# Block-sparse attention and routed experts on one core: sparse weighing one tick later, and three early weight subtractions moved from GpSimd to VectorE

## The chip, the cores and the metric

The kernel runs on 1 core of one Trainium2 chip. The metric is the device time of one execution in microseconds (us), smaller being better. The kernel before was timed three times: 539.57 us is the median, 537.37 and 539.88 us the ends.

## What is computed

Attention with a block mask, followed by a layer of eight experts of which each token uses one. The shapes are q, k, v of 4 x 8 x 768 x 64 and, for the experts, 3072 tokens of 512 numbers, eight pairs of weights of 512 x 1024 and 1024 x 512, all in fp32.

```
scores = (q @ k^T) / 8                     # per batch and head, 768 x 768
mask   = |blk_i - blk_j| <= 1, or blk_i or blk_j is the first or last block,
         or blk_j is one of 3 sampled blocks of blk_i          # blocks of 32
x      = softmax(scores where mask) @ v    # -> 3072 tokens x 512
logits = x @ w_gate + modality_bias[modality_id]
e      = argmax(logits);  g = softmax(logits)[e]
out    = g * (relu(x @ w1[e]) @ w2[e])
```

## The kernel before

**Attention, by items and ticks.** The queries of the first and last block see all keys; they make 16 dense items (`"d"`, one of a batch and a pair of heads each). All others see eight blocks of 32 keys; they make 88 sparse items (`"s"`). Four sparse items (two places n, two batches b) make one tile of 128 tokens, so there are 22 sparse tiles, here called tile 0 to tile 21. The items stand in one list, `items`, of NI = 104. Each goes through steps named by a letter, and a table `LAG` (line 59) says how many ticks after its place in the list an item's step is written into the program:

- S, scores on TensorE (line 532, two items at once); M, mask and row minimum on VectorE (line 540); X, exponentials on ScalarE (line 548); T, four transposes on TensorE (line 557); A, copy of the transposes out of PSUM on ScalarE (line 562).
- For the last item of a tile only: W, the products with the values that all four items share, on TensorE (line 579); V, the row sums (line 572) and the products with each item's own three sampled blocks (line 588); O, the division that copies the output tile `xr` out of PSUM on VectorE (lines 439 to 441); Y, four transposes of that tile (line 595) with a copy on ScalarE (line 597); G, the gate's products (line 605), after which the tokens are routed and the tile is written to DRAM (line 1221).

The order within a tick is the string `ORDER` (line 60): O X T S M G V A Y W. There is no other scheduler: each engine executes in the order that this loop writes, and semaphores hold it where data or a buffer is missing. `hook` (line 1186) is called at eight places of a tick and issues the loads: the values of a tile (`fetch_v`, line 484, at `VL`; `fetch_own`, line 510, at `VG`) go through the one queue of SyncE (SP), and `share_v` (line 499) copies values between the two value buffers on GpSimd.

**Early weights.** Once 16 of the 24 tiles of tokens are routed, a first group of 256 tokens of one expert is chosen, and the generator `early_groups` (line 787) is advanced once a tick beside the attention. It loads pieces of that expert's weights in halves of 256 KB (line 710) into staging buffers and splits each piece in two: ScalarE copies it with rounding to fp32r (`split`, line 721), and a subtraction gives the rest (line 722). `POOL_SPLITS` (line 80) lists the pieces whose subtraction goes to GpSimd instead of VectorE. Pieces 0, 1 and 2 are split at ticks 6, 9 and 12 of that generator, and pieces 3 and 4 after the attention's last loads. Each product with weights is three matmuls (high by high, high by low, low by high), lines 746 to 748 and 761 to 763.

**Experts.** Groups of 256 tokens follow each other: gather by indirect DMA (line 728), transposes (line 735), first layer, ReLU, second layer, scatter (line 782). The first group's products start as soon as the last attention products are issued.

Of the kernel before, what the change touches and what calls it, by code (L numbers as in the profile page):

```python
# [9 lines left out]
F32 = mybir.dt.float32  # L10
# [5 lines left out]
ALU = mybir.AluOpType  # L16
# [5 lines left out]
B, H, S, D = 4, 8, 768, 64  # L22
# [33 lines left out]
START_TICKS = 14  # L56
DENSE_DVE = ((0, 0), (0, 1))
DENSE_AFTER = (21, 29, 45, 47)
LAG = {'d': {'S': 0, 'M': 1, 'X': 2, 'T': 4, 'A': 4, 'W': 7, 'O': 8, 'V': 101, 'Y': 11, 'G': 13}, 's': {'S': 0, 'M': 1, 'X': 2, 'T': 4, 'A': 4, 'W': 5, 'V': 7, 'O': 8, 'Y': 10, 'G': 13}}
ORDER = 'OXTSMGVAYW'  # L60
ADVANCE = (((2, 3), (6, 6), (7, 1)), ((0, 2), (1, 1), (6, 4)))
LHS = (6, 5)
# [3 lines left out]

KL = (-2, 2)
QP = (-2, 2)
VL = (8, 1)
VS = (11, 7)  # L70
VG = ((9, 6), (10, 3))

DENSE_IN = ((19, 14, 30), (49, 38, 44))
Q_IN = 22
# [2 lines left out]
XD = (7, 7)  # L77
TAIL = 7
EVAC_DVE = ()
POOL_SPLITS = (1, 2, 4, 7, 15, 16, 21)  # L80

TICKS = (6, 9, 12)
DOWN0 = ((9, 5), (9, 7), (14, 7), (12, 9), (13, 9), (13, 9), (17, 9), (15, 10))
# [5 lines left out]
def attention_moe(ctx, tc, kD, qD, qH, v0, v1, blocks, modality, w_gate, bias, w1, w2, out):  # L89
    nc = tc.nc  # L90
# [28 lines left out]
    with ExitStack() as actx:  # L119
# [529 lines left out]
        stg, wh, wl, xg, xh, xl, hh, hl, og = [], [], [], [], [], [], [], [], []  # L649
# [40 lines left out]
        NSTG, NRING, LOOK_D, LOOK_S = 5, 5, 6, 4  # L690
# [9 lines left out]
        def staged(n):  # L700
            return stg[(0, 1, 0, 1, 0, 1, 0, 2)[n] if n < 8 else n % NSTG]
# [14 lines left out]
                src = w2[bass.ds(e, 1), 2 * c * P:(2 * c + 2) * P, :].rearrange("e (k p) f -> p (e k) f", p=P)  # L716
                nc.sync.dma_start(staged(n).rearrange("p (k f) -> p k f", k=2), src)

        def split(n, eng=None):
            h, l = wh[n % NRING], wl[n % NRING]  # L720
            nc.scalar.copy(h, staged(n))  # L721
            (eng or (nc.gpsimd if n in POOL_SPLITS else nc.vector)).tensor_tensor(l, staged(n), h.bitcast(F32), ALU.subtract)  # L722

        def gather(g):
            assert all(tau in written for tau in range(TES[g] if g < NEAR else NT))
# [60 lines left out]

        def early_groups():
            now = {"fetch": 0, "split": 0, "gather": 0, "column": 0, "half": 0}

            def load(nf, ns, slow=False):  # L790
                while True:
                    f, p = now["fetch"], now["split"]
                    if p < ns and p < f:
                        split(p)
                        now["split"] += 1
                    elif f < nf and f - NSTG < p and (f < 8 * NEAR or known):
                        if slow or now["half"]:
                            fetch(f, now["half"])
                            now["half"] ^= 1
                        else:  # L800
                            fetch(f)
                        now["fetch"] += not now["half"]
                        if slow:
                            return
                    else:
                        return

            def rows(g):
                if now["gather"] == g and ready[g] and (g != 1 or tail[1]) and (g or settled()):
                    if g == 1:  # L810
                        expert_slots(8)
                    gather(g)
                    now["gather"] += 1

            def columns(g):
                for n in range(2):
                    if now["column"] == 2 * g + n and now["gather"] > g:
                        column(g, n, bank())
                        now["column"] += 1
                        return  # L820

            expert_slots(0)
            tick, wait = 0, 0
            while not tail[0]:
                rows(0)
                if now["gather"]:
                    wait += 1
                    if wait > 4:
                        columns(0)
                p = sum(tick >= x for x in TICKS)  # L830
                load(p + 2, p, True)
                tick += 1
                yield "tick"
            expert_slots(2, 5, 6, 7)
            while now["column"] < 2:
                rows(0)
                columns(0)
            load(10, 5)
            for k in range(4):
                o = bank()  # L840
                for c in range(4):
                    for f in (2 * k, 2 * k + 1):
                        up(0, c, f, o)
                    rows(1)
                    yield
                relu(k, o)
            o = [bank() for _ in range(2)]
            for f in range(8):
                load(*DOWN0[f])
                for t in range(2):  # L850
                    down(0, f, t, o[t])
                    rows(1)
                    yield
                if f in (3, 7):
                    columns(1)
            while not tail[1]:
                yield
            rows(1)
            for t in range(2):
                give(0, t, o[t])  # L860
            while now["column"] < 4:
                columns(1)
            o = [bank() for _ in range(4)]
            for c in range(4):
                load(*UP1[c])
                for f in range(8):
                    up(1, c, f, o[f // 2])
                    if f % 2:
                        rows(2)
                        yield  # L870
            for k in range(4):
                relu(k, o[k])
            turned_low.append(True)
            o = [bank() for _ in range(2)]
            for f in range(8):
                load(*DOWN1[f])
                for t in range(2):
                    down(1, f, t, o[t])
                    rows(2)
                    yield  # L880
                if f in (5, 6):
                    columns(2)
            for t in range(2):
                give(1, t, o[t])
            while not ready[2]:
                yield
            rows(2)
            load(22, 17)
            while now["column"] < 6:
                columns(2)  # L890
            load(22, 20)
# [281 lines left out]
        items = list(dense[0])  # L1173
# [5 lines left out]
        NI = len(items)  # L1179
# [24 lines left out]
        tail = [False, False]  # L1204
# [38 lines left out]
        for g in range(2 * NM):  # L1243
            half, m = divmod(g, NM)
            t = at["s", half, m, 0, 0]
# [88 lines left out]
        with man:  # L1334
# [16 lines left out]
            while t < NI + LAG["s"]["G"] + 1 or fillers or slots_todo or choosers or early:  # L1351
                spot = 0
                for op in ORDER:
                    if op in "TSMAXOW":
                        hook(spot)
                        spot += 1
                    for kind in "ds":
                        k = t - LAG[kind][op]
                        if 0 <= k < NI and items[k][0] == kind:
                            do(op, items[k])  # L1360
                hook(7)
                if t >= NI:
                    tail[0], tail[1] = t >= NI + TAIL, t >= NI + LAG["s"]["V"]
                    for _ in range(2):
                        advance(2)
                        while slots_todo:
                            slot_lhs(nc.vector if len(slots_todo) % 2 else nc.gpsimd)
                        step(choosers, 1)
                        step(early, 1)
                t += 1  # L1370
# [59 lines left out]
```

## Time and profile before

| | |
|---|---|
| median of three runs | 539.57 us |
| the profiled execution's own time | 542.68 us |
| its span, first to last instruction | 541.0 us |
| TensorE (PE) busy | 514.5 us, 95% |
| VectorE (DVE) busy | 379.0 us, 70% |
| ScalarE (ACT) busy | 335.7 us, 62% |
| GpSimd (POOL) busy | 223.2 us, 41% |
| scores of the last sparse items (last line 532) | begin at 216.85 us |
| first product with weights (first line 746) | begins at 236.94 us |

The profile tells one execution. Times in it are counted from the span's start. PE is TensorE's matmuls, PEld its weight loads, SPq the DMA queue of SyncE. A row of the timeline has the start, the duration, the engine, the line, the operation, what it writes and reads, and the count; in square brackets stands how long the engine was idle before it and what ended that, where "issue" is a wait that no semaphore of the profile explains. Matmuls overlap at their ends, so the distance from one row's start to the next is the better measure of what a group costs.

### The profile page before, as it was taken

To read this page: it belongs to the slowest core of one execution; us is meant where nothing else is said; L and a number is where in the kernel's file an instruction comes from. 1 tells how busy PE (TensorE), PEld (TensorE's weight loads), DVE (VectorE), ACT (ScalarE), POOL (GpSimd) and SP (SyncE) were. 2 spreads that over 40 slices of the span, in tenths; PEclk is the share of its full clock that TensorE was granted. 3 is DMA by queue.
4 is the path that set the end of the run, shared out by engine and by line. 5 is a ranking of instruction groups with operands and counts; after the bars stand their busy time and mean duration, and the time that the engine had idled before them with its cause. 6 is when DMAs were issued, how large, how long until landed. Compare 5 with 4: busy or idle time off the path is not lost.

```text
span 541.0 us, 19019 instructions
## 1 busy us (share of the span) xinstructions
PE 514.5 (95%) x7298; PEld 433.6 (80%) x7298; DVE 379.0 (70%) x1136; ACT 335.7 (62%) x765; POOL 223.2 (41%) x454
## 2 busy tenths in 40 slices
PE   7999899988999999789999999999999999999995
PEld 5667677766778677678889898998989899898984
DVE  7985588667779799966996656656566565656553
ACT  4689777877888878744445554545455554555552
POOL 3578574656558775640455031130303213030213
PEclk9999999999999999899999999999999999999999
DMA  7994986989757779646778875767758667675840
GB/s 282 335 249 147 244 247 187 238 225 236 188 161 209 196 202 274 174 143 250 265 247 287 291 240 197 256 209 230 247 175 268 186 237 235 209 257 177 256 154 22
DMA packets 49443, 119.44 MB, mean 221 GB/s; under 512 B 7744, under 2 KB 8128, under 8 KB 49344
## 3 DMA queue, kind: packets, MB, share of 16 engines
q1 hardware_dynamic: 45248, 105.02, 64.2%
q0 software_dynamic: 4096, 13.12, 6.9%
q8 instruction: 59, 0.97, 0.8%
q14 instruction: 40, 0.33, 0.2%
HBM read 105.52 MB, written 12.86 MB: 219 GB/s over the span
## 4 chain that ended last, share of the span: by engine, by line
issue 40%; PE 35%; DVE 10%; POOL 6%; DMA 5%; ACT 2%; SPq 1%; POOLq 0%; DVEq 0%; ACTq 0%
PE bank L532 6%; PE bank L557 6%; PE bank L579 3%; PE bank L588 3%; POOL slot L728 3%; DMA out<-slot,si 2%; POOL out L782 2%; PE bank L432 2%; PE bank L605 2%; DVE y L540 1%; PE bank L762 1%; PE bank L410 1%; PE bank L763 1%; PE bank L761 1%; PE bank L595 1%
## 5 line engine op out<-in xcount | busy, mean ns | idle before, releaser
L722 DVE TENSOR_TENSOR slot<-slot 128x1024 fp32r<-128x1024 f32 x96 | 119.4, 1248 | 89.7 <-ACT slot L721 87.9
L721 ACT CAST slot<-slot 128x1024 fp32r<-128x1024 f32 x104 | 108.0, 1048 | 101.9 <-PE bank L747 52.0
L748 PE MATMUL bank<-slot 128*128 128x256 f32 x384 | 107.8, 281 | 0.7 <-DVE slot L722 0.7
L746 PE MATMUL bank<-slot 128*128 128x256 f32 x384 | 108.4, 282 | 0.0
L747 PE MATMUL bank<-slot 128*128 128x256 f32 x384 | 107.6, 280 | 0.0
L782 POOL DMA_INDIRECT out<-slot,si x20 | 25.4, 1270 | 178.6 <-ACT slot L778 175.5
L548 ACT ACTIVATE a<-y,mn 128x256 f32<-128x256 f32 x176 | 88.7, 511 | 10.6 <-DVE mn L540 10.3
L761 PE MATMUL bank<-slot 128*128 128x512 f32 x192 | 76.6, 399 | 0.0
L762 PE MATMUL bank<-slot 128*128 128x512 f32 x192 | 75.9, 395 | 0.0
L763 PE MATMUL bank<-slot 128*128 128x512 f32 x192 | 75.7, 394 | 0.0
L748 PEld LDWEIGHTS bank<-slot 128*128 128x128 f32 x384 | 72.2, 188 | 0.9 <-DVE slot L722 0.9
L746 PEld LDWEIGHTS bank<-slot 128*128 128x128 f32 x384 | 72.2, 188 | 0.6
L747 PEld LDWEIGHTS bank<-slot 128*128 128x128 f32 x384 | 72.1, 188 | 0.4
L540 DVE CUSTOM_DVE_ANT_1 y<-bank,smask 128x256 f32<-128x256 f32 x176 | 66.3, 417 | 0.4
L481 POOL COPY slot<-slot 128x128 f32 x264 | 64.3, 298 | 0.0
L562 ACT COPY at<-bank 128x512 f32<-128x512 f32 x88 | 50.7, 578 | 12.6 <-PE bank L557 12.5
L557 PE MATMUL bank<-ident,a 128*128 128x128 f32 x352 | 53.2, 282 | 3.9 <-DVE mn L540 1.9
L532 PE MATMUL bank<-slot,q_raw 64*32 64x256 f32 x1408 | 51.0, 382 | 2.8 <-issue 2.0
L503 POOL TENSOR_SCALAR slot<-slot 32x1024 f32<-32x1024 f32 x40 | 41.8, 1045 | 24.8 <-PE bank L588 10.6
L557 PEld LDWEIGHTS bank<-ident,a 128*128 128x128 f32 x352 | 38.5, 141 | 8.9 <-issue 2.9
L763 PEld LDWEIGHTS bank<-slot 128*128 128x128 f32 x192 | 36.1, 188 | 8.4
L762 PEld LDWEIGHTS bank<-slot 128*128 128x128 f32 x192 | 36.1, 188 | 7.8 <-DVE slot L722 0.4
(302 smaller groups left out, 863.3 us busy)
## 6 DMA issues: line engine op xcount, KB each, us to landing
slot<-w SPq DMA_DIRECT2D x100, 512.0 KB, 3.8
slot<-v SPq DMA_DIRECT2D x180, 128.0 KB, 4.1
x_d<-xr SPq DMA_DIRECT2D x22, 256.5 KB, 5.6
q_raw<-qH SPq DMA_DIRECT2D x22, 256.0 KB, 5.1
slot<-v SPq DMA_DIRECT2D x16, 256.0 KB, 4.8
slot<-kD SPq DMA_DIRECT2D x13, 256.0 KB, 4.1
slot<-v SPq DMA_DIRECT2D x4, 768.0 KB, 14.9
slot<-w SPq DMA_DIRECT2D x10, 256.0 KB, 3.9
```

Of the source, the lines that this page charges most:

```text
L532: nc.tensor.matmul(sp[u][32 * pr:32 * pr + 32, b * 256:(b + 1) * 256], lhsT=q[r, b * NPAIR + pr, n, :], rhs=kv[r, s0:s0 + 8, b, pr, :], st ...
L540: nc.vector.tensor_tensor_reduce(y[:, u, :].rearrange("p (s f) -> p s f", s=8), sp[u][:, b * 256:(b + 1) * 256].rearrange("p (s f) -> p s ...
L548: nc.scalar.activation(a[:, u, :], y[:, u, :], AF.Exp, bias=mn[:, u:u + 1], scale=-1.0, accum_out=total[:, u:u + 1])
L557: nc.tensor.transpose(tp[:, k:k + P], a[:, u, c * P:(c + 1) * P], ident)
L721: nc.scalar.copy(h, staged(n))
L722: (eng or (nc.gpsimd if n in POOL_SPLITS else nc.vector)).tensor_tensor(l, staged(n), h.bitcast(F32), ALU.subtract)
L746: nc.tensor.matmul(o, lhsT=h[:, fs], rhs=xh[g % 2][:, c, :], start=c == 0 and f % 2 == 0, stop=False)
L747: nc.tensor.matmul(o, lhsT=h[:, fs], rhs=xl[g % 2][:, c, :], start=False, stop=False)
L748: nc.tensor.matmul(o, lhsT=l[:, fs], rhs=xh[g % 2][:, c, :], start=False, stop=c == 3 and f % 2 == 1)
L761: nc.tensor.matmul(o, lhsT=hh[0][:, f, ts_], rhs=h[:, fs], start=f == 0, stop=False)
L762: nc.tensor.matmul(o, lhsT=hh[0][:, f, ts_], rhs=l[:, fs], start=False, stop=False)
L763: nc.tensor.matmul(o, lhsT=hl[f // 4][:, f % 4, ts_], rhs=h[:, fs], start=False, stop=f == 7)
```

## The change

Sparse items' W goes from lag 5 to 6, V from 7 to 8, O from 8 to 9, Y from 10 to 11; G stays at 13. The very last item keeps the old lags (`LAST`). The loads of values move with it by one tick (`VL`, `VG`; `VS` stays). Pieces 1, 2 and 4 leave `POOL_SPLITS`, so their subtractions are VectorE's. While `early_groups` runs beside the attention, the subtraction of a split piece is put off to the generator's next tick (`lows`), and no fetch is issued in the tick of a split.

```
-LAG = {'d': {... 'W': 7, 'O': 8, 'V': 101, 'Y': 11, 'G': 13}, 's': {... 'A': 4, 'W': 5, 'V': 7, 'O': 8, 'Y': 10, 'G': 13}}
+LAG = {'d': {... 'W': 7, 'O': 8, 'V': 101, 'Y': 11, 'G': 13}, 's': {... 'A': 4, 'W': 6, 'V': 8, 'O': 9, 'Y': 11, 'G': 13}}
+LAST = {'W': 5, 'V': 7, 'O': 8, 'Y': 10}
...
-VL = (8, 1)
+VL = (9, 1)
 VS = (11, 7)
-VG = ((9, 6), (10, 3))
+VG = ((10, 6), (11, 3))
...
-POOL_SPLITS = (1, 2, 4, 7, 15, 16, 21)
+POOL_SPLITS = (7, 15, 16, 21)
...
-        def split(n, eng=None):
-            h, l = wh[n % NRING], wl[n % NRING]
-            nc.scalar.copy(h, staged(n))
-            (eng or (nc.gpsimd if n in POOL_SPLITS else nc.vector)).tensor_tensor(l, staged(n), h.bitcast(F32), ALU.subtract)
+        def split(n, eng=None, rest=None):
+            h, l, s = wh[n % NRING], wl[n % NRING], staged(n)
+            nc.scalar.copy(h, s)
+
+            def low():
+                (eng or (nc.gpsimd if n in POOL_SPLITS else nc.vector)).tensor_tensor(l, s, h.bitcast(F32), ALU.subtract)
+
+            if rest is None:
+                low()
+            else:
+                rest.append(low)
...
                     if p < ns and p < f:
-                        split(p)
+                        split(p, rest=lows if slow else None)
                         now["split"] += 1
+                        if slow:
+                            return
...
             while not tail[0]:
+                while lows:
+                    lows.pop()()
                 rows(0)
...
+                    if op in LAST and t - LAST[op] == NI - 1:
+                        do(op, items[NI - 1])
...
-                    tail[0], tail[1] = t >= NI + TAIL, t >= NI + LAG["s"]["V"]
+                    tail[0], tail[1] = t >= NI + TAIL, t >= NI + LAST["V"]
```

On TensorE, one period of four ticks (one sparse tile) late in the attention. Before, from the scores of line 532 to the gate (605), the shared products (579) and the transposes (557, 595):

```order
L532 MATMUL bank<-slot,q_raw 32x256 x16
L572 MATMUL bank<-rexp,fold 32x8 x4
L588 MATMUL bank<-slot,at 32x64 x32
L557 MATMUL bank<-ident,a 128x128 x8
L532 MATMUL bank<-slot,q_raw 32x256 x16
L605 MATMUL bank<-wg_raw,xT 64x8 x8
L579 MATMUL bank<-slot,at 64x64 x16
L557 MATMUL bank<-ident,a 128x128 x4
L595 MATMUL bank<-ident,xr 128x128 x4
L557 MATMUL bank<-ident,a 128x128 x4
```

The same engine and period in the changed kernel, whose lines are one higher there (533 for 532, 558 for 557, and so on):

```order
L558 MATMUL bank<-ident,a 128x128 x4
L533 MATMUL bank<-slot,q_raw 32x256 x16
L606 MATMUL bank<-wg_raw,xT 64x8 x8
L558 MATMUL bank<-ident,a 128x128 x4
L580 MATMUL bank<-slot,at 64x64 x16
L558 MATMUL bank<-ident,a 128x128 x4
L533 MATMUL bank<-slot,q_raw 32x256 x16
L596 MATMUL bank<-ident,xr 128x128 x4
L558 MATMUL bank<-ident,a 128x128 x4
L573 MATMUL bank<-rexp,fold 32x8 x4
L589 MATMUL bank<-slot,at 32x64 x32
```

The work is the same. Before, the transposes stand in two runs (eight together, and four, four, four); in the changed kernel they stand in four runs, with the shared products, the own products and the scores between them, and the shared products no longer follow the gate. Counted in the same way over the program from the first shared products to the first product with weights, runs of transposes go from 54 to 95, and places where the gate is followed at once by the shared products from 12 to 1.

On VectorE, at the mask of the items whose scores are the last but one (540, which order calls ISA), with a tile's gate and routing (608, 294, 297, 302) and the choice of the second early group (1024, 1027) ahead of it. Before:

```order
L608 TENSOR_TENSOR lg<-bank,btok 128x8
L294 TENSOR_REDUCE mx<-lg 128x2
L297 TENSOR_TENSOR dl<-lg,mx 128x16
L1024 TENSOR_REDUCE cm_6058<-cc_5865 128x1
L1027 SCALAR_TENSOR_TENSOR ce_6060<-cc_5865,cm_6058,desc 128x8
L302 SCALAR_TENSOR_TENSOR eq<-dl,desc 128x16
L540 ISA y,mn<-bank,smask 128x256
L540 ISA mn 128x1
```

The same place in the changed kernel (line 725 is line 722 before):

```order
L609 TENSOR_TENSOR lg<-bank,btok 128x8
L295 TENSOR_REDUCE mx<-lg 128x2
L298 TENSOR_TENSOR dl<-lg,mx 128x16
L1039 TENSOR_REDUCE cm_6036<-cc_5836 128x1
L1042 SCALAR_TENSOR_TENSOR ce_6038<-cc_5836,cm_6036,desc 128x8
L303 SCALAR_TENSOR_TENSOR eq<-dl,desc 128x16
L725 TENSOR_TENSOR slot<-slot 128x1024
L541 ISA y,mn<-bank,smask 128x256
L541 ISA mn 128x1
```

The subtraction of piece 1, before on GpSimd between two calls of `share_v`, now stands in VectorE's row ahead of a mask. Piece 2's subtraction is moved in the same way, four masks later, and piece 4's follows piece 3's on VectorE. On SyncE, the first half of a staging buffer's next piece waits for the subtraction that frees it, as before; what stands behind it there are the six loads of own value rows of the last two sparse tiles. Before, the last tile's six stood three and three around the second half of piece 4; now both halves of piece 4 stand ahead of all six.

More of the change, by code (lines that the diff above doesn't have):

```diff
@@ L58 @@
 DENSE_AFTER = (21, 29, 45, 47)
-LAG = {'d': {'S': 0, 'M': 1, 'X': 2, 'T': 4, 'A': 4, 'W': 7, 'O': 8, 'V': 101, 'Y': 11, 'G': 13}, 's': {'S': 0, 'M': 1, 'X': 2, 'T': 4, 'A': 4, 'W': 5, 'V': 7, 'O': 8, 'Y': 10, 'G': 13}}
+LAG = {'d': {'S': 0, 'M': 1, 'X': 2, 'T': 4, 'A': 4, 'W': 7, 'O': 8, 'V': 101, 'Y': 11, 'G': 13}, 's': {'S': 0, 'M': 1, 'X': 2, 'T': 4, 'A': 4, 'W': 6, 'V': 8, 'O': 9, 'Y': 11, 'G': 13}}
+LAST = {'W': 5, 'V': 7, 'O': 8, 'Y': 10}
 ORDER = 'OXTSMGVAYW'
@@ L788, in early_groups @@
             now = {"fetch": 0, "split": 0, "gather": 0, "column": 0, "half": 0}
+            lows = []
             def load(nf, ns, slow=False):
@@ L833, in early_groups @@
                 yield "tick"
+            while lows:
+                lows.pop()()
             expert_slots(2, 5, 6, 7)
```

## Prediction

> **What bounds the kernel now.** I read the page first, for the span and the engines.
>
> ```profile
> span 541.0 us, 19019 instructions
> PE 514.5 (95%) x7298; PEld 433.6 (80%) x7298; DVE 379.0 (70%) x1136; ACT 335.7 (62%) x765; POOL 223.2 (41%) x454
> q8 instruction: 59, 0.97, 0.8%
> ```
>
> TensorE (PE) is the bound as a whole: 95% busy. A change in the attention shows only through PE's time up to the first product with weights at 236.94 us; behind 241 us PE has no idle row until the last group. So I took PE's groups from 30 to 236 us, the stretch that the change touches (duration and mean; then idle time ahead and its releasers).
>
> ```profile
> L557 PE MATMUL bank<-ident,a 128*128 128x128 f32 x352 | 53.2, 282 | 3.9 <-DVE mn L540 1.9 <-ACT xT L597 1.1 <-issue 0.7
> L532 PE MATMUL bank<-slot,q_raw 64*32 64x256 f32 x1328 | 48.4, 382 | 2.3 <-issue 2.0 <-PE bank L557 0.2
> L579 PE MATMUL bank<-slot,at 128*64 128x64 f32 x704 | 26.7, 225 | 3.6 <-issue 1.9 <-ACT at L562 1.7
> L588 PE MATMUL bank<-slot,at 128*32 128x64 f32 x1351 | 24.3, 220 | 2.1 <-issue 2.1
> L605 PE MATMUL bank<-wg_raw,xT 128*64 128x8 f32 x352 | 14.2, 205 | 0.9 <-issue 0.9
> ```
>
> Idle time ahead of these is 3.9 + 2.3 + 3.6 + 2.1 + 0.9 = 12.8 us of 206. Of it 7.6 us is "issue". Then PE's timeline in an undisturbed stretch, to see whether PE is the limit there or is kept waiting.
>
> ```profile
> 152.54 0.66 PE L557 MATMUL bank<-ident,a 128*128 128x128 f32 x4
> 153.13 1.09 PE L532 MATMUL bank<-slot,q_raw 64*32 64x256 f32 x32
> ...
> 159.12 1.09 PE L557 MATMUL bank<-ident,a 128*128 128x128 f32 x8
> 160.14 1.09 PE L532 MATMUL bank<-slot,q_raw 64*32 64x256 f32 x32
> 161.17 0.64 PE L605 MATMUL bank<-wg_raw,xT 128*64 128x8 f32 x16
> 161.74 0.25 PE L572 MATMUL bank<-rexp,fold 128*32 128x8 f32 x8
> ...
> 162.83 0.66 PE L595 MATMUL bank<-ident,xrd 128*128 128x128 f32 x4
> 163.32 1.04 PE L557 MATMUL bank<-ident,a 128*128 128x128 f32 x8
> 164.29 1.09 PE L532 MATMUL bank<-slot,q_raw 64*32 64x256 f32 x32
> 165.31 0.64 PE L605 MATMUL bank<-wg_raw,xT 128*64 128x8 f32 x16
> 165.80 1.13 PE L579 MATMUL bank<-slot,at 128*64 128x64 f32 x32
> ```
>
> No row has a wait, and each group begins before the one ahead has ended. Here the order of the groups on PE is itself the time: a longer order is paid in full.
>
> **The order on PE, the first term.** From start to start, four transposes between other groups take 153.13 - 152.54 = 0.59 us, eight 160.14 - 159.12 = 1.02, twelve (with the turned tile) 164.29 - 162.83 = 1.46. So a transpose costs 0.11 us and each run of them 0.14 us more, for entering and leaving. The changed order has 41 more runs (95 for 54). Two stand behind the last scores, where PE waits anyway; 39 x 0.14 = 5.5 us remain. The gate takes 161.74 - 161.17 = 0.57 us where another group follows and 165.80 - 165.31 = 0.49 where the shared products follow; that pair goes 11 times: 0.9 us. Together PE has 6.4 us more to do, 0.3 us a tile. The work is otherwise the same, so this can't be below nothing; how much of it is seen depends on the next two terms.
>
> **What the later lag takes away.** These are the rows of PE with idle time that has a releaser, and one of the issue kind.
>
> ```profile
> 37.94 1.15 PE L579 MATMUL bank<-slot,at 128*64 128x64 f32 x30 [0.50 <-ACT at L562]
> 65.14 0.66 PE L557 MATMUL bank<-ident,a 128*128 128x128 f32 x4 [1.10 <-ACT xT L597]
> 80.99 0.28 PE L430 MATMUL bank<-su,ident 128*64 128x1 f32 x4 [0.52 <-DVE mn L540]
> 95.59 0.44 PE L410 MATMUL bank<-ident,a 128*128 128x128 f32 x2 [0.58 <-ACT a L400]
> 125.01 0.97 PE L579 MATMUL bank<-slot,at 128*64 128x64 f32 x25 [1.28 <-issue]
> 222.42 0.63 PE L557 MATMUL bank<-ident,a 128*128 128x128 f32 x4 [1.67 <-DVE mn L540]
> 235.66 1.35 PE L588 MATMUL bank<-slot,at 128*32 128x64 f32 x64 [0.77 <-issue]
> 241.05 0.38 PE L748 MATMUL bank<-slot 128*128 128x256 f32 x1 [0.71 <-DVE slot L722]
> ```
>
> The shared products at 37.94 wait for ScalarE's copy, which a tick more covers: 0.50. The other three waits in the first half, 1.10 + 0.52 + 0.58, either lose their releaser or are filled by a PE that comes later. I take all four, -2.7 us, between -0.5 (only the first) and -2.7.
>
> **The pauses.** At 125.01 PE stopped inside one group, after 7 of 32 matmuls, where nothing new has to be ready. Such pauses are the 7.6 us of issue, less 0.77 at 235.66: 6.8 us in about ten places. The instruction queue (q8) moved 59 packets; PE's 7298 matmuls with as many weight loads make 247 a packet. The five groups above are 4087 matmuls, so 33 packets, and 6.4 us over these are 0.19 us each. If a pause is a packet that comes late, a PE that takes 0.19 us longer over a packet waits so much less for the next: 10 x 0.19 = -1.9 us. The ends are 0 (pauses have nothing to do with PE's pace) and -6.4 (PE goes at the pace of its instructions). The Trainium skill, Runtime: NRT & Kernel Launch, section Instruction fetch mechanics, says that instructions come in blocks of 256 and that crossing a block's end is mostly hidden; the packet count agrees with the size, but by "hidden" the pauses would have another cause, and this term would be 0.
>
> **Behind the last scores.** From 216.85 us PE has some 12 us of work and takes until 236.94. What holds it:
>
> ```profile
> 208.92 1.23 DVE L722 TENSOR_TENSOR slot<-slot 128x1024 fp32r<-128x1024 f32 x1 [0.42 <-ACT slot L721]
> 216.66 2.35 POOL L722 TENSOR_TENSOR slot<-slot 128x1024 fp32r<-128x1024 f32 x1 [3.09 <-ACT slot L721]
> 216.71 2.33 DVE L1027 SCALAR_TENSOR_TENSOR ce<-cc,cm,desc 128x8 f32<-128x8 f32 x1
> 219.04 0.36 SPq L710 DMA_DIRECT2D slot<-w  x1
> 219.10 2.17 POOL L503 TENSOR_SCALAR slot<-slot 32x1024 f32<-32x1024 f32 x2
> 220.28 1.01 DVE L318 TENSOR_SCALAR gs<-gs 128x2 f32<-128x2 f32 x1
> 224.53 2.36 POOL L722 TENSOR_TENSOR slot<-slot 128x1024 fp32r<-128x1024 f32 x1 [3.26 <-PE bank L605]
> 224.92 2.02 DVE L566 TENSOR_TENSOR rexp<-sums,quad 128x32 f32<-128x32 f32 x1
> 226.92 0.36 SPq L710 DMA_DIRECT2D slot<-w  x1
> 229.51 1.31 SPq L520 DMA_DIRECT2D slot<-v  x3
> ...
> 226.00:227.00 1.00, 1.00 (x9) 0.88 (x7) 1.00 (x2) 0.34 (x1) 0.91 (x2) 0.50 0.85 279
> ...
> 228.00:229.00 1.00, 1.00 (x7) 1.00 (x6) 0.94 (x2) 0.78 (x3) 0.92 (x2) 0.50 0.78 158
> ```
>
> Two small VectorE operations of 8 and 32 elements took 2.33 and 2.02 us: each ended with the GpSimd subtraction that began before it. On VectorE such a subtraction takes 1.23 us. So VectorE is held about 4 us less for pieces 1 and 2 and gets 2 x 1.23 = 2.5 us of work. The 1.67 us at 222.42 should go.
>
> But that isn't what ends this stretch. The last own products (235.66) wait for value rows, and these stand in SyncE's queue behind the weight half at 226.92, which waited for the subtraction that ended at 224.53 + 2.36 = 226.89. From the first weight half (219.04, right behind the subtraction that ended at 219.01) the queue then runs almost without a break to 229.51 + 1.31 = 230.82, and PE starts 4.84 us later. In the changed kernel piece 1's subtraction stands in VectorE's row behind a division, a mask and six small operations, where before they were held for 2.2 us; adding 1.23 us in place of that hold, and the 1 us hold by line 503 (as at 220.28) that now can come earlier, puts its end at 218.4 to 219.9, for 219.01. So I take 0 for the last own products, between -1.0 and +1.0.
>
> With PE done sooner and the rows not, PE stands idle for some 4 us ahead of them. After the gaps at 222.42 and just behind, the granted clock (third from the end in the windows) read 0.50 from 226 to 229 us. If that follows a longer gap too, 3 us at half clock fall on products with weights that nothing covers: +1.5; if not, 0. I take half, +0.8.
>
> The 0.71 us at 241.05 is piece 3's subtraction, held behind GpSimd's of piece 4; that one is now VectorE's, and stands behind piece 3's: -0.7. Piece 4 is needed only in the second layer, several us later, which hides its 1.2 us; without that cover it would cost these.
>
> **The sum.** 6.4 - 2.7 - 1.9 + 0 + 0.8 - 0.7 = +1.9 us: 544.6 for the profiled execution's own 542.68 us. Against the median, 3.1 us lower, this is 541.5 us, 0.35% more. About 0.5%, 2.7 us, is what a measurement of this kernel can tell from no change.
>
> **The rivals.**
>
> *Faster.* PE's pace is set by when its instructions come: the pauses take up the whole order cost. The last value rows also come 1.0 us sooner, and the clock stays up: 6.4 - 6.4 - 2.7 - 1.0 - 0.7 = -4.4 us: 535.2. For it: 6.8 us of pauses are enough to hold 6.4. Against it: from 150 to 172 us there is no pause at all.
>
> *Slower, order in full.* The pauses don't give, only the first wait goes, the clock halves: 6.4 - 0.5 - 0.7 + 1.5 = +6.7 us: 546.3. For it: the undisturbed stretch above. It decides if PE shows as much issue time as before.
>
> *Slower, held subtractions.* VectorE's subtraction is held in its turn by the copies of line 503 (2.17 us for two at 219.10), before the queue of SyncE can go on: the last own products come up to 2.2 us later, +1.9 + 2.2 = +4.1 us: 543.7. It decides if piece 1's subtraction ends later than 219.9. The Trainium skill, SBUF — State Buffer, section Who interferes with whom, has a rule that speaks for it: a VectorE instruction with two inputs in SBUF contends with a GpSimd instruction that reads SBUF, and the one that starts first holds the other off. The rows at 216.71 and 224.92 agree as to the hold; no row before shows a subtraction held by line 503.
>
> **Chances and range.** The forecast 0.40 (its own range 538.5 to 542.2), faster 0.28, slower by order 0.22, slower by held subtractions 0.10. So faster by over 0.5% is 0.28, within it 0.40, slower 0.32. The range 534.5 to 546.0 leaves out about a third of the faster case and half of the slower one, 0.2 in all.
>
> **What would show it.** Right: isolated fours of transposes at 0.57 to 0.59 us all through the attention, the last scores beginning 1 to 3 us later than 216.85; no 2 us VectorE operation beside a GpSimd subtraction; an idle row of over 3 us ahead of the last line 588, with the clock at 0.50 behind it; no wait ahead of the matmuls with piece 3's low part. Wrong: last scores at 214 us or sooner with little issue time (faster), or at 221 us or later (order in full). If the last own products come with no wait, the queue of SyncE wasn't what ended the stretch.

## The result, and the profile after

The changed kernel takes 542.19 us (median of 16 runs, 538.73 to 544.82), the kernel before 537.42 us (16 runs, 532.95 to 540.88): 1.0078 times as long, with a 95% interval of 1.0057 to 1.0100. That is slower by 0.8%, some 4.2 us. The forecast was 541.5 us with "within 0.5%" as the likeliest case; the time lies in the range, but the change is larger than the forecast's +1.9 us: it falls among the slower cases, which together had a chance of 0.32. The kernel before has a lower median over these runs than over the three shown before (539.57 us), so that its profiled execution (542.68 us) lay 5.3 us above it. The profiled execution of the changed kernel took 542.61 us, close to its own median.

From the page of the changed kernel, the span and the engines:

```profile
span 540.9 us, 19025 instructions
PE 519.3 (96%) x7298; PEld 433.2 (80%) x7298; DVE 376.7 (70%) x1139; ACT 335.5 (62%) x765; POOL 214.4 (40%) x451
```

TensorE is busy 4.8 us longer for the same 7298 matmuls, in a span of the same length; 3.6 us of this lie between 30 and 236 us (194.65 us for 191.03). Its groups there (busy time, mean ns; then idle time ahead of them):

```profile
L558 PE MATMUL bank<-ident,a 128*128 128x128 f32 x352 | 56.4, 284 | 1.3 <-DVE xr L442 0.5 <-ACT at L563 0.4 <-DVE mn L541 0.3
L533 PE MATMUL bank<-slot,q_raw 64*32 64x256 f32 x1336 | 47.0, 382 | 1.4 <-POOL slot L482 0.6 <-DVE xrd L452 0.5 <-ACT a L401 0.3
L580 PE MATMUL bank<-slot,at 128*64 128x64 f32 x704 | 25.6, 225 | 0.3 <-issue 0.3
L589 PE MATMUL bank<-slot,at 128*32 128x64 f32 x1407 | 25.6, 220 | 4.4 <-DMA slot<-v 3.2 <-issue 1.2
L606 PE MATMUL bank<-wg_raw,xT 128*64 128x8 f32 x352 | 14.1, 205 | 0.0
```

The transposes (558, formerly 557) went from 53.2 to 56.4 us; the other groups moved by 1.4 us at most, up or down. The idle time of these five groups fell from 12.8 to 7.4 us, and of what is left 3.2 us is one new wait, for value rows. TensorE's timeline around the last scores:

```profile
212.26 0.66 PE L558 MATMUL bank<-ident,a 128*128 128x128 f32 x4
212.84 1.09 PE L533 MATMUL bank<-slot,q_raw 64*32 64x256 f32 x32
...
214.44 0.66 PE L558 MATMUL bank<-ident,a 128*128 128x128 f32 x4
215.02 1.15 PE L580 MATMUL bank<-slot,at 128*64 128x64 f32 x32
...
216.10 0.66 PE L558 MATMUL bank<-ident,a 128*128 128x128 f32 x4
216.69 1.09 PE L533 MATMUL bank<-slot,q_raw 64*32 64x256 f32 x32
...
232.99 0.27 PE L589 MATMUL bank<-slot,at 128*32 128x64 f32 x2 [1.45 <-DMA slot<-v]
235.05 1.28 PE L589 MATMUL bank<-slot,at 128*32 128x64 f32 x62 [1.78 <-DMA slot<-v]
...
237.03 0.56 PE L754 MATMUL bank<-slot 128*128 128x256 f32 x1
```

Every run of four transposes takes 0.58 or 0.59 us to the next group's start. The last scores begin at 216.69 us (before: 216.85). Ahead of the last own products TensorE stands idle for 1.45 + 1.78 = 3.2 us, and the first product with weights begins at 237.03 (before: 236.94). VectorE, the queue of SyncE, and the microseconds behind the idle time (third number from the end: granted clock):

```profile
215.60 0.23 DVE L1042 SCALAR_TENSOR_TENSOR ce<-cc,cm,desc 128x8 f32<-128x8 f32 x1
216.07 1.23 DVE L725 TENSOR_TENSOR slot<-slot 128x1024 fp32r<-128x1024 f32 x1 [0.16 <-issue]
```

```profile
225.97 0.92 SPq L711 DMA_DIRECT2D slot<-w  x2
227.07 2.83 SPq L521 DMA_DIRECT2D slot<-v  x6
```

```profile
236.00:237.00 1.00, 1.00 (x19) 0.84 (x9) 0.63 (x2) 0.00 (x0) 0.00 (x0) 0.53 0.09 16
237.00:238.00 1.00, 1.00 (x6) 1.00 (x5) 0.13 (x2) 0.53 (x2) 0.92 (x1) 0.50 0.00 0
238.00:239.00 1.00, 1.00 (x7) 1.00 (x6) 0.00 (x0) 1.00 (x3) 0.69 (x2) 0.50 0.30 49
```

The small operation that took 2.33 us takes 0.23, and piece 1's subtraction ends at 217.30. The last value rows still follow two weight halves and are all issued at 229.90; TensorE goes on 5.1 us later, and then at half clock.

**One reckoning for all kernels.** Behind the first product with weights every profiled execution of this study needs 302.9 to 304.2 us, whatever the kernel. So the time is decided between the first scores and that product. I split this stretch of TensorE in three. "Idle" is the sum of the times in brackets of TensorE's timeline there. "Half clock" is what the lower clock cost: one less the granted clock, added up over windows of 1 us up to the first product with weights. "Own" is the rest: what the order of the instructions takes at full clock. Each is from one profiled execution; the last column is from 8 to 16 timed runs, each kernel against runs of the kernel before in the same session; the sessions weren't all on the same chip. It leaves out runs over 1.5% above the fastest of the same kernel (two of splits_only, three of splits_rows, one each of paired_rows and regrouped), which the medians given below keep, and the quotient of two medians can differ from it by 0.2%. Times are in us.

| kernel | lag | runs of transposes | own | idle | half clock | ratio to before (95%) |
|---|---|---|---|---|---|---|
| before | old | 54 | 196.8 | 14.9 | 1.7 | 1 |
| before_again | old | 54 | 194.9 | 10.9 | 5.1 | one run |
| splits_only | old | 54 | 196.6 | 8.2 | 0.0 | 0.9931 (0.9887 to 0.9975) |
| splits_rows | old | 54 | 194.7 | 7.1 | 0.0 | 0.9938 (0.9905 to 0.9971) |
| pool_only | old | 54 | 197.1 | 11.9 | 0.0 | 0.9945 (0.9912 to 0.9978) |
| order_only | old | 91 | 200.6 | 9.9 | 1.1 | 1.0026 (1.0001 to 1.0051) |
| splits_order | old | 91 | 199.0 | 7.4 | 3.4 | 0.9986 (0.9950 to 1.0022) |
| changed kernel | later | 95 | 201.6 | 11.3 | 0.5 | 1.0078 (1.0057 to 1.0100) |
| lag_only | later | 95 | 201.6 | 8.4 | 1.7 | 1.0076 (1.0043 to 1.0108) |
| rows_first | later | 95 | 201.6 | 10.1 | 1.7 | 1.0023 (0.9990 to 1.0056) |
| paired | later | 56 | 197.2 | 9.9 | 8.2 | 1.0075 (1.0043 to 1.0106) |
| paired_rows | later | 56 | 198.4 | 11.8 | 1.7 | 1.0011 (0.9983 to 1.0039) |
| regrouped | later | 56 | 197.0 | 13.3 | 3.4 | 1.0040 (1.0005 to 1.0075) |
| regrouped_rows | later | 56 | 198.5 | 10.7 | 1.7 | 1.0038 (1.0004 to 1.0073) |

### The profile page after: what moved, and what is told of

Its sections match the earlier page's. It is cut to its first block, busy times and chain, and to the rows that moved or that the text cites. A ratio compares the mean times of both kernels' runs of the same rounds, so it can differ in the third digit from the quotient of the medians.

```text
span 540.9 us, 19025 instructions
## 1 busy us (share of the span) xinstructions
PE 519.3 (96%) x7298; PEld 433.2 (80%) x7298; DVE 376.7 (70%) x1139; ACT 335.5 (62%) x765; POOL 214.4 (40%) x451
## 4 chain that ended last, share of the span: by engine, by line
issue 39%; PE 37%; DVE 9%; POOL 5%; DMA 5%; ACT 3%; SPq 1%; POOLq 0%; ACTq 0%; DVEq 0%
PE bank L533 7%; PE bank L558 6%; PE bank L589 3%; PE bank L580 3%; DMA out<-slot,si 2%; POOL slot L736 2%; PE bank L596 2%; PE bank L606 2%; POOL out L790 2%; PE bank L433 2%; DVE y L541 2%; DMA slot<-v 1%; PE bank L754 1%; PE bank L411 1%; PE bank L770 1%
## 5 line engine op out<-in xcount | busy, mean ns | idle before, releaser
L725 DVE TENSOR_TENSOR slot<-slot 128x1024 fp32r<-128x1024 f32 x99 | 122.6, 1244 | 91.7 <-ACT slot L722 89.7
L558 PE MATMUL bank<-ident,a 128*128 128x128 f32 x352 | 56.4, 284 | 1.3 <-DVE xr L442 0.5
L533 PE MATMUL bank<-slot,q_raw 64*32 64x256 f32 x1408 | 49.4, 382 | 1.9 <-POOL slot L482 0.6
```

The costliest lines, as they stand in the source:

```text
L533: nc.tensor.matmul(sp[u][32 * pr:32 * pr + 32, b * 256:(b + 1) * 256], lhsT=q[r, b * NPAIR + pr, n, :], rhs=kv[r, s0:s0 + 8, b, pr, :], st ...
L558: nc.tensor.transpose(tp[:, k:k + P], a[:, u, c * P:(c + 1) * P], ident)
```

## The experiments

The theory at the start was the prediction's: the changed order costs TensorE its own time, and the waits and pauses give part of it back. Its rivals: the value rows that come late; the subtractions that hold or free VectorE; and, formed on the way, that the later lag itself makes waits.

### before_again: the kernel before, unchanged, for a second profile

> The kernel before, unchanged, for a second profile of it: its first profiled execution took 542.68 us, 5.3 us over the median of its 16 runs (537.42), so its trace may hold pauses that a usual run lacks. If the pauses of the issue kind vary from run to run, this profile has fewer than the 7.6 us of the first on TensorE from 30 to 236 us, and the last scores begin before 216 us. If they belong to the kernel, about 7 us again, and a time near 542.

One run, 541.41 us, own time 194.9 us. TensorE's idle rows around the last scores:

```profile
217.79 0.43 PE L588 MATMUL bank<-slot,at 128*32 128x64 f32 x16 [1.88 <-issue]
223.53 1.98 PE L579 MATMUL bank<-slot,at 128*64 128x64 f32 x32 [2.44 <-POOL slot L503]
```

```profile
219.00:220.00 1.00, 1.00 (x6) 0.72 (x4) 1.00 (x4) 1.00 (x2) 0.00 (x0) 0.50 0.97 268
...
226.00:227.00 1.00, 1.00 (x7) 1.00 (x6) 0.00 (x0) 0.37 (x1) 0.92 (x2) 0.50 0.07 23
```

Neither wait was in the first profile. Of the first profile's four waits with a releaser in the first half, the largest (1.10 us) and that of 0.52 are gone here, and so is the 1.67 us behind the last scores. From 218 to 228 us the clock is halved, which alone cost 5.1 us. The issue idle fell from 8.0 to 4.6 us, and the last scores begin at 213.48 us, so the pauses do vary, as one half of the expectation has it, though the time is near the 542 us of the other half. So a wait or a pause in one profile of this kernel needn't be one of the kernel.

### lag_only: the later lag alone (edit of the changed kernel)

```
-POOL_SPLITS = (7, 15, 16, 21)
+POOL_SPLITS = (1, 2, 4, 7, 15, 16, 21)
...
-                        split(p, rest=lows if slow else None)
+                        split(p)
                         now["split"] += 1
-                        if slow:
-                            return
```

> Only the later lag (W, V, O, Y and the loads of values); the subtractions stay on GpSimd as before. Theory (order cost on TensorE: 41 more runs of transposes at 0.14 us): 3.5 to 6 us slower than before, as slow as the whole change or slower. Rival (the subtractions and the rows behind them cost the time): within 1.5 us of before.

542.46 us (12 runs), 1.0076 times before: as slow as the whole change. The lag, with the order on TensorE that comes with it, is what made the kernel slower; how much of it is the order, order_only and the runs behind it ask. In its profile the last scores begin at 217.69 us, and TensorE waits little for the last value rows:

```profile
232.94 0.27 PE L589 MATMUL bank<-slot,at 128*32 128x64 f32 x2 [0.21 <-DMA slot<-v]
233.82 1.13 PE L589 MATMUL bank<-slot,at 128*32 128x64 f32 x62 [0.61 <-DMA slot<-v]
```

### splits_only: the subtractions alone, with the old lags (edit of the changed kernel)

```
-LAG = {... 's': {... 'W': 6, 'V': 8, 'O': 9, 'Y': 11, 'G': 13}}
+LAG = {... 's': {... 'W': 5, 'V': 7, 'O': 8, 'Y': 10, 'G': 13}}
...
-VL = (9, 1)
+VL = (8, 1)
...
-VG = ((10, 6), (11, 3))
+VG = ((9, 6), (10, 3))
```

> Only the subtractions on VectorE, put off by a tick; the lags stay as before, and so does TensorE's order (54 runs of transposes). Theory (order cost): between 2 us faster and 1 us slower than before, since VectorE is no longer held by the GpSimd subtractions, and the last value rows end the stretch as before. Rival (the subtractions and the rows behind them): 3 to 5 us slower.

535.22 us (8 runs), 0.9931: faster by 0.7%, about 3.7 us on the 538.2 us that the kernel before had in that session, and so faster than either theory had it. TensorE's only waits of note behind the last scores are short, and from the first scores to 530 us the clock isn't halved:

```profile
218.91 1.15 PE L580 MATMUL bank<-slot,at 128*64 128x64 f32 x30 [1.50 <-ACT at L563]
228.16 1.05 PE L589 MATMUL bank<-slot,at 128*32 128x64 f32 x60 [0.53 <-DMA slot<-v]
```

The two halves don't add up: -3.7 and +4.1 us would make +0.4, and together they make +4.2. With intervals of about 2.4, 1.7 and 1.2 us to either side, this gap of 3.8 us is only just clear of noise.

### pool_only: the list of GpSimd's subtractions alone (edit of the kernel before)

```
-POOL_SPLITS = (1, 2, 4, 7, 15, 16, 21)
+POOL_SPLITS = (7, 15, 16, 21)
```

> The kernel before with pieces 1, 2 and 4 taken out of the list of GpSimd's subtractions and nothing else: no subtraction is put off, lags and loads as before. Theory 'hold' (what the splits gain is that GpSimd's subtractions no longer hold VectorE for 2 us): the whole of the splits' gain, 534.5 to 536 us, ratio 0.993 to 0.996. Theory 'put off' (the gain comes from the subtraction standing a tick later, behind the mask that TensorE waits for): no gain or a loss, 537.5 to 539.5 us, ratio 0.999 to 1.003.

535.66 us, 0.9945, with nothing put off: the theory "put off" falls, and the gain is what "hold" asked for. It has a rival that this run leaves standing: the subtraction on VectorE is also shorter (1.23 us for 2.35), so that piece 1's ends at 215.84 us here, for 219.01 before, and the queue of SyncE goes on sooner. What is left of the hold shows on VectorE, beside line 503 on GpSimd:

```profile
214.61 1.23 DVE L722 TENSOR_TENSOR slot<-slot 128x1024 fp32r<-128x1024 f32 x1 [1.18 <-ACT slot L721]
...
217.21 1.01 DVE L1027 SCALAR_TENSOR_TENSOR ce<-cc,cm,desc 128x8 f32<-128x8 f32 x1
```

```profile
216.04 2.17 POOL L503 TENSOR_SCALAR slot<-slot 32x1024 f32<-32x1024 f32 x2 [5.19 <-DMA slot<-x_d,gi_e]
```

The operation of eight elements ends at 218.22 and the copies at 218.21: now one copy holds it where a subtraction of 2.35 us had.

### order_only: the scores ahead of the transposes, on the kernel before

```
-ORDER = 'OXTSMGVAYW'
+ORDER = 'OXSTMGVAYW'
```

> The kernel before, with the scores written ahead of the transposes in each tick (one letter of the order string moved): 91 runs of transposes for 54, gate followed by shared products as before, lags, loads and subtractions as before. Theory 'order' (each further run of transposes costs PE 0.09 to 0.14 us): 37 x 0.09 to 37 x 0.14 = +3.3 to +5.2 us on the kernel before, ratio 1.006 to 1.010. Theory 'late rows' (what the later lag cost is that the last tile's own value rows come behind later weight halves, and the half clock behind that wait; the order on PE is hidden by pauses): within 1 us of before, ratio 0.998 to 1.002.

540.67 us (before: 538.28), 1.0026: between the two theories, slower by 0.1 to 2.7 us. Its timeline at 156 us shows the term itself, a four alone in 0.59 us:

```profile
156.33 0.66 PE L557 MATMUL bank<-ident,a 128*128 128x128 f32 x4
156.92 1.09 PE L532 MATMUL bank<-slot,q_raw 64*32 64x256 f32 x32
157.94 0.66 PE L557 MATMUL bank<-ident,a 128*128 128x128 f32 x4
```

TensorE's own time is 200.6 us for 194.9 and 196.8 in the two profiles of before; its idle time and half clock are 11.0 for 16.0 and 16.6. The order costs TensorE what was worked out. Waits take part of it up, but less than these profiles say, because those of before lay 3 and 5 us above their medians and this one lies at its own.

### splits_order: the same, on the kernel with the fewest waits

```
-ORDER = 'OXTSMGVAYW'
+ORDER = 'OXSTMGVAYW'
```

(on splits_rows, below)

> The subtractions' part with the last tile's own rows early (534.9 us, the run with the fewest waits on TensorE, 7.1 us up to the first product with weights and no half clock), with the scores now ahead of the transposes: 91 runs for 54. In the profile, TensorE's time up to the first product with weights less its idle time and half clock was 195 to 197 us in kernels of 54 to 56 runs and 200 to 202 in those of 91 to 95. Theory 'paid in full where little waits': +4.6 us of own time and about as much in the time, 539 to 540 us, ratio to before 1.001 to 1.004. Theory 'order is absorbed' (the scores first cost 1.4 us on the kernel before): +1.4, 536.3 us, ratio 0.995 to 0.998.

537.80 us, 0.9986, for 0.9938 without the letter's move. The two were timed in different sessions, each against before; the difference of the ratios is 0.0048, 2.6 us. That is between the two theories again. In the profiled run one new wait, for GpSimd's copies, carries a good part of it:

```profile
221.47 1.98 PE L580 MATMUL bank<-slot,at 128*64 128x64 f32 x32 [2.92 <-POOL slot L504]
```

```profile
219.00:220.00 1.00, 0.00 (x0) 0.00 (x0) 1.00 (x5) 0.39 (x1) 0.76 (x1) 1.00 1.00 266
220.00:221.00 1.00, 0.00 (x0) 0.00 (x0) 1.00 (x6) 1.00 (x2) 0.92 (x2) 0.52 0.99 256
```

The clock went down while TensorE still waited.

### rows_first: the changed kernel, with the last own value rows issued early

```
             for n in range(2):
+                if g == 2 * NM - 1:
+                    side(last(g - 2) + VL[0], vg[n], VL[1])
+                    continue
                 side(last(g - 2) + VG[n][0], vg[n], VG[n][1])
```

> The changed kernel, with the last tile's own value rows issued right behind its shared ones, ahead of the two weight halves that held them in SyncE's queue. Theory 'late rows': the waits of 1.45 and 1.78 us ahead of the last own products go, and with them the half clock (some 3 us at half speed, 1.5 us): -3.2 to -4.7 us, 537.5 to 539 us, ratio to before 1.000 to 1.003. Theory 'order': PE had lost its time before; the waits go but the weight halves, now behind the rows, hold the first product with weights about as long: -1 to 0 us, 541 to 542 us, ratio 1.006 to 1.008.

539.47 us, 1.0023 for the changed kernel's 1.0078: 3.0 us less, close to what "late rows" asked for. The intervals, 0.9990 to 1.0056 and 1.0057 to 1.0100, just don't meet. The queue and TensorE:

```profile
220.76 5.08 SPq L521 DMA_DIRECT2D slot<-v  x6
...
228.02 3.11 SPq L521 DMA_DIRECT2D slot<-v  x6
231.37 0.90 SPq L711 DMA_DIRECT2D slot<-w  x2
```

```profile
235.72 1.21 PE L589 MATMUL bank<-slot,at 128*32 128x64 f32 x62 [1.49 <-DMA slot<-v]
```

The rows now go ahead of the weight halves, and one wait of 1.49 us remains of 3.2, with no half clock behind it. What still holds them is ahead of them: tile 20's own rows (220.76 to 225.84). A second cause is read from the kernel and not shown by a wait: the buffer is one of two, so that it is free only when the own products of tile 19, one tick later than with the old lag, are done.

### splits_rows: the subtractions alone, with these rows early

The edit of rows_first, on splits_only.

> The subtractions' part alone (lags as before), with the last tile's own value rows issued right behind its shared ones. In the splits alone the last own products waited 0.53 us for these rows and no half clock followed. Both theories: -0.5 us on the 535.2 us of the splits alone, 534 to 535.5 us, ratio to before 0.990 to 0.995. A third theory, that any move of these loads ahead of the weight halves makes the weights late: +1 to +2 us, 536 to 537 us.

534.91 us (12 runs), 0.9938, no different from splits_only. Here the rows come long before they are needed, and the last own products have no wait:

```profile
217.12 2.83 SPq L521 DMA_DIRECT2D slot<-v  x6
```

```profile
224.29 1.28 PE L589 MATMUL bank<-slot,at 128*32 128x64 f32 x64
```

This and splits_only are the fastest versions found, 0.6 to 0.7% under the kernel before; pool_only can't be told from them.

### paired and paired_rows: the changed kernel with eight transposes together

```
-                        if 0 <= k < NI and items[k][0] == kind:
-                            do(op, items[k])
+                        for late in (1, 0) if kind == "s" and op in "TA" else (None,):
+                            j = k - (late or 0)
+                            if 0 <= j < NI and items[j][0] == kind and (late is None or items[j][-1] == 1 - late):
+                                do(op, items[j])
```

(paired_rows has the edit of rows_first as well.)

> The whole change, but the transposes and their copies of the first item of each pair one tick later, so that eight transposes stand together: 56 runs instead of 95, with the later lag kept. Theory (order cost): 39 x 0.14 = 5.5 us less than the changed kernel, less what pauses or waits give back: 2 us faster to 1 us slower than before. Rival (the later lag itself, or the subtractions): as slow as the changed kernel, 3 to 5 us over before.

> The changed kernel with eight transposes together (56 runs for 95) and the last tile's own value rows issued early. Theory 'late rows' alone: as rows_first, 537.5 to 539 us. Theory 'order' as well as late rows: 39 x 0.09 = 3.5 us less than rows_first, 534 to 536 us, ratio to before 0.993 to 0.997. If neither is it, as the paired kernel without the early rows: 541 to 542 us, ratio 1.006 to 1.008.

541.76 us, 1.0075, and 539.78 us, 1.0011: not what "order" asked for; the second is nearest to "late rows" alone. Own time fell to 197.2 and 198.4 us, so the runs of transposes did cost it; but the time is that of the changed kernel, and with the early rows that of rows_first. The sparse transposes and copies of the first of each two items stand a tick later here, so that eight transposes follow each other. In paired's profile waits came in its place, the longest at 119 us:

```profile
119.37 1.15 PE L589 MATMUL bank<-slot,at 128*32 128x64 f32 x62 [2.48 <-issue]
```

```profile
118.00:119.00 1.00, 0.00 (x0) 0.00 (x0) 0.24 (x2) 1.00 (x4) 0.00 (x0) 1.00 1.12 281
...
121.00:122.00 1.00, 1.00 (x32) 0.30 (x16) 0.96 (x5) 0.35 (x1) 0.92 (x2) 0.50 1.01 188
...
126.00:127.00 1.00, 1.00 (x22) 0.97 (x20) 0.00 (x0) 0.86 (x4) 1.00 (x5) 0.50 0.92 250
```

The clock is halved from 120 to 127 us, behind the pause of 2.48 us. It is halved again from 215 to 222 us, behind three pauses of 0.50, 0.51 and 0.48 us between 213 and 215 us.

### regrouped and regrouped_rows: the changed kernel with 56 runs by the order string

```
-ORDER = 'OXTSMGVAYW'
+ORDER = 'OXSGYTMVAW'
```

(regrouped_rows has the edit of rows_first as well.) No transpose and no copy is put off here.

> The changed kernel with the order string O X S G Y T M V A W, so that the later lag has 56 runs of transposes for 95, and no transpose or copy is put off. Theory 'order': TensorE's own time falls by 4 to 5 us to 196 to 197.5, and the time by as much less what the waits take back: 537.5 to 540 us, ratio to before 0.999 to 1.003. Theory 'the lag itself' (two value buffers and masks that come later against TensorE's pace: the paired kernel had its own time at 196.8 and lost it again in waits): 541 to 542.5 us, ratio 1.005 to 1.009.

> The changed kernel with that order string and the last tile's own value rows issued early. Theory 'order': 2 to 3 us less than regrouped, 535 to 537 us, ratio to before 0.994 to 0.999. Theory 'the lag itself': as the paired kernel with early rows, 539 to 540.5 us, ratio 1.001 to 1.005.

540.93 us, 1.0040, and 539.93 us, 1.0038: the first between the two theories, the second as "the lag itself" has it. Own time is down to 197.0 and 198.5; idle and half clock are 16.7 and 12.4 us. Two rows of regrouped and one of regrouped_rows stand for many:

```profile
215.84 0.80 PE L580 MATMUL bank<-slot,at 128*64 128x64 f32 x20 [1.36 <-issue]
221.42 0.35 PE L589 MATMUL bank<-slot,at 128*32 128x64 f32 x9 [1.32 <-issue]
```

```profile
221.19 0.25 PE L573 MATMUL bank<-rexp,fold 128*32 128x8 f32 x8 [2.02 <-DVE mn L541]
```

## Why the prediction was right, and where it was wrong

**The order on PE (+6.4).** The mechanism was right, the size a little high. In the nine profiles with 54 or 56 runs the own time is 194.7 to 198.5 us, 196.8 on average; in the five with 91 or 95 it is 199.0 to 201.6, 200.9 on average. The two groups don't touch; 4.1 us between them is 0.11 us a run, for 0.14 from the timeline, and within either lag the difference is 3.8 us, 0.10 a run. What the time shows of it is less: 0.26% and 0.48% (1.4 and 2.6 us) with the old lags. With the later lag, 56 runs against 95 can't be told apart: the ratios with 56 are 1.0011 to 1.0075, those with 95 1.0023 to 1.0078. In the profiles with the later lag, 95 runs have 3.8 us more own time, but 2.2 us less issue idle and 2.5 us less half clock.

**What the later lag takes away (-2.7).** This step failed, and it decided the result. ScalarE's releasers did fall, from 4.0 to 1.2 us of idle time in the two profiles, as argued. The waits for masks fell too. But new waits took their place: value rows 3.2 us and `hoh` (an operand that VectorE makes for the early group's row numbers), 1.5 us for 0.2. All idle time with a releaser went from 6.9 to 8.3 us between the two profiles, where 2.7 us less was forecast. At equal runs of transposes the later lag costs time: the three kernels with VectorE's subtractions, old lags and 54 runs average 0.9938, the four with the later lag and 56 runs 1.0041, 1.0% or 5.5 us more. In their profiles TensorE's own time is 1.6 us longer, idle time 2.3 (11.4 for 9.1) and half clock 3.8 (3.8 for 0). Nearly all of the longer idle time is of the issue kind (5.3 for 3.2 us); that with a releaser is 6.1 for 5.9. Two limits: paired and regrouped also move other steps, and at many runs, with the rows early, the lag costs less than noise (rows_first 1.0023 for splits_order's 0.9986, intervals that overlap). I had priced a step that stands further behind as only slack. By the kernel's text it also uses its buffer a tick longer, so what refills the buffer comes later, while the very last item keeps its old place; the runs show this for the last value rows alone.

**The pauses (-1.9).** Open. Issue idle is 2.0 to 3.5 us in the five profiles with more runs and 2.2 to 8.0 in the nine with fewer, 3.0 and 4.8 on average: the size that I took, and so within either lag (1.7 and 2.2 us less). But it went from 8.0 to 3.1 us between the two profiled executions, and from 8.0 to 4.6 between two profiles of the same kernel, so the mechanism isn't shown.

**The profiled execution against the median.** Between the two profiled executions the sum reads: own +4.8, idle -3.6, half clock -1.2, the part behind -0.2, the part ahead +0.2, together 0.0 us, for +1.9. But I subtracted the surplus of before's execution over the median as a constant, while it was made, in part, of the very waits that I counted as gains. By the constant part behind the first product with weights, an execution of before at its median would have some 12 us of idle time and half clock (an estimate: 537.4 less 1.7 outside the span, less 304.1, less 23.7 ahead of the first scores, less own time of 195.8) where the profiled one had 16.6; the changed kernel has 11.8 in an execution at its median. By this estimate nothing was left to give back at the median, and the own time came through.

**Behind the last scores (0, and +0.8 for the clock).** The chain was read rightly: the queue of SyncE ends this stretch. The idle time ahead of the last own products came at 3.2 us, with half clock behind it, and rows_first shows its price, 3.0 us. The half clock, most of it behind the first product with weights, cost no more than before's own (1.7 us by windows in both), which the sum had left out; so +0.8 should have been 0.

**Held subtractions.** Right that VectorE is freed: 0.23 us for 2.33. Too small in the sum: I put nothing on it but 0.7 for piece 3's wait, which is gone as forecast. The edit alone is worth 3.0 us (pool_only), by the hold or by the sooner queue. In the changed kernel it was worth nothing (1.0076 without it, 1.0078 with it): by the profiles TensorE comes 1.0 us sooner to the last scores (216.69 us for lag_only's 217.69), and then waits 3.2 us for the last value rows, which don't, where lag_only waits 0.8. The rival with held subtractions didn't occur; piece 1's ended at 217.30, not after 219.9. The rule that it leaned on (the Trainium skill, SBUF — State Buffer, section Who interferes with whom: a VectorE instruction with two inputs in SBUF and a GpSimd instruction that reads SBUF hold each other off, whichever starts second waiting) agrees with pool_only's 1.01 us beside line 503.

**The rivals.** "Order in full" asked for last scores at 221 us or later: they came at 216.69. The forecast's own sign, last scores 1 to 3 us later than 216.85, didn't come either; between the two profiles idle time had taken up the order by then. "Faster" asked for a PE whose pauses take up the whole order; the own time shows in the result. The range held in part by luck: two errors of opposite sign, on the lag and on the subtractions, met in the sum. That the time came within 0.7 us of 541.5 is luck as well: the median of three runs that the forecast stood on was 2.1 us above that of 16. In size the change is nearest to the rival with held subtractions (+4.1 us), whose mechanism wasn't there.

What stays open is why the later lag at 56 runs has more idle time. The value rows are one part that was shown (rows_first; paired_rows against paired), though regrouped gained nothing by it. The most lies in pauses that no semaphore explains; the rest at masks, at `hoh` and at GpSimd's copies, in other places in each profile. A third value buffer would test the rest; it wasn't tried.

## What to carry to other kernels

Before counting a wait as a gain, profile the same kernel twice, or compare the profiled execution with the median: here what was above the median was made of such waits and of lost clock, and they weren't there to be won. Split a saturated engine's stretch into own time, idle time and lost clock; an edit of the order is read from the first, and the time says how much of it the second took up. A step that is moved later holds its buffers longer: follow what refills them, and the queue that this stands in, before calling the move free.

## What the runs showed of the hardware that was not expected

The clock halved after short idle times on TensorE. Every single wait of 2.0 us or more ahead of the first product with weights was followed, or accompanied, by a granted clock of 0.50 (2.02, 2.05, 2.18, 2.33, 2.44, 2.48 and 2.92 us; at the 2.44 it had been halved before); waits of 1.5 to 1.9 us sometimes were (1.88 in before_again) and sometimes weren't (1.50 in splits_only). The length of one wait isn't the whole rule: three pauses of about 0.5 us within 2 us were followed by it in paired, and three like them in lag_only (from 211 to 213 us) weren't. It then lasted some 3 to 10 us, so that a wait can cost more than twice its length (before_again: 1.88 and 2.44 us of waits, and 5.1 us of half clock). The Trainium skill, TensorE: Matmul & The Clock Gate, section HAM oscillation — how this bites in real kernels, warns of idle gaps over about 3.4 us; the measured gaps here are shorter.

One execution of the same kernel differs from another by up to 8 us (532.95 to 540.88 us in the 16 runs of the kernel before). In the fourteen profiled executions, whose spans go from 529.0 to 542.4 us, nearly all of the difference lies ahead of the first product with weights: what follows it takes 302.9 to 304.2 us in every one.
